# Softmax sums of a whole batch in the PSUM banks of the next batch's k and v projections

## The chip, the core and the metric

The kernel runs on one core of one Trainium2 chip. A core has five engines, each with its own instruction queue that runs in order: TensorE (PE, matrix products; its weight loads are shown apart as PEld), VectorE (DVE, elementwise work), ScalarE (ACT, activation functions and copies), GpSimd (POOL, here almost only the issuer of loads) and SyncE (SP, which issues the other transfers). Sixteen DMA engines move the data that the queues ask for. SBUF is the working memory of 128 partitions; PSUM, of eight banks, takes the results of PE. The metric is the device time of one execution in microseconds, lower is better. Three runs of the kernel before took 473.25, 474.64 and 474.59 us; the median is 474.59.

## What is computed

Linformer attention over 8 batches of 8 heads, 1024 tokens and 64 features a head, followed by a feed-forward block with a squared relu.

```python
k_proj = np.einsum('ks,bhsd->bhkd', E, k)          # 64 projected keys
v_proj = np.einsum('ks,bhsd->bhkd', F, v)
scores = scale * np.matmul(q, k_proj.transpose(0, 1, 3, 2))
attn = np.exp(scores - max); attn = attn / (np.sum(attn, axis=-1, keepdims=True) + 1e-09)
x = np.matmul(attn, v_proj)                        # -> (8192, 512)
h = np.maximum(x @ w_in, 0.0)                      # (8192, 2048)
out = h * h @ w_out                                # (8192, 512)
```

E and F are 64 x 1024, w_in 512 x 2048, w_out 2048 x 512; all inputs and the output are float32. The kernel multiplies in bfloat16 and leaves out the subtraction of the maximum.

## The kernel before, in words

Most of the work is the feed-forward block. Both of its products are done with seven half-size products in place of eight (Strassen's scheme in Winograd's form), with the sums of blocks made on DVE. A batch has two chunks of 512 tokens; the first product of a chunk has four groups (class Group) of seven partial products (p1, p5, p4, p6, p2, p3, p7), each of four matmuls of 256 columns. The generator `firsts` yields after each partial product, `seconds` does the same for the second product (`second_spread`), and `both` puts one of each side by side: a step is four matmuls of a first product and four of a second one. A chunk takes 28 steps, a batch 56.

Attention is threaded between the steps. `plan` maps a step's number to the stages that are put behind that step's products; `on(step, b, name)` enters a method of the batch's Attention object, and in the loop over b the number t = 56 (b - 1) + 28 is the base of the steps in which batch b + 1 is finished and batch b + 2 begun. The order of PE is that of the program text (`manual_schedule`); the order of all other queues is found by a planner, which sorts instructions by when it expects them to be ready. Batches 0 and 1 are done in a different way, before and at the start of this loop (the `chunk_` methods); batches 2 to 7 use these stages:

- `load_q`, `load_kv`: 1 MB each of q, k and v, from memory by POOL's queue, cast to bfloat16 on the way. There is one buffer each for Q, K and V.
- `transpose_q_dma`: Q to qT by a transposing DMA from SP's queue (one qT buffer).
- `project`: sixteen matmuls of 512 columns; those of k go to partitions 0 to 63 of the first bank of a PSUM pair, those of v to partitions 64 to 127 of the second bank. `keep_k` and `keep_v` copy them out, `transpose_k_dma` makes kT.
- `scores(pr)`, for head pair pr of 0 to 3: two matmuls of 512 columns into the PSUM pair, and one exp of 1024 columns on ACT into an expT tile (four buffers).
- `sums_spread(pr)`, for two head pairs at once: eight matmuls with 32 columns of ones as weights, each on its own 64 x 32 piece of the array, into the PSUM pair; Ln and Exp(-x) of 128 x 1024 on ACT give 1/sum in `inv`; and eight DMAs of 32 partitions x 4 KB from SP's queue copy it to the rows where it is needed, in two `rs` tiles.
- `values(pr)`: four matmuls of 64 x 64 x 512 columns into the PSUM pair, and two multiplies by `rs` on DVE into xT.

There is one such PSUM pair (tag "pair", two banks, ps_att) in this part of the program: a stage that writes it waits until the last reader of the stage before is through. `rs` and `inv` share a tag with three buffers.

For batch b + 1 and the next one the loop has: scores 3 at t + 1, sums of pairs 2 and 3 at t + 3, values at t + 7, 10, 20 and 23; Q of b + 2 is loaded from t + 11, behind the last values multiply so far, and transposed at t + 26, k and v of b + 2 are projected at t + 28, its scores 0 to 2 stand at t + 44, 47 and 53, its sums of pairs 0 and 1 at t + 50.

The loads of v of batch 0 stand ahead of the weights' loads in the kernel before and in the changed one.

Of the kernel before, what the change touches and what calls it, by code (L numbers as in the profile page):

```python
# [1 line left out]

# [7 lines left out]
P = 128  # L10
F32 = mybir.dt.float32
BF16 = mybir.dt.bfloat16
AF = mybir.ActivationFunctionType
ALU = mybir.AluOpType
PE = mybir.EngineType.PE
LO, HI = slice(0, 64), slice(64, 128)
# [3 lines left out]
def kernel(  # L20
# [11 lines left out]
    nc = tc.nc  # L32

    B, H, S, D = q.shape
    KP = E.shape[0]
# [4 lines left out]
    NI = 8  # L40
# [4 lines left out]
    TCH = S // 2  # L45
# [10 lines left out]
    const_pool = ctx.enter_context(tc.tile_pool(name="const", bufs=1))  # L56
# [4 lines left out]
    soft_pool = ctx.enter_context(tc.tile_pool(name="soft", bufs=3))  # L61
# [10 lines left out]
    def pair_psum(n, shape, dtype):  # L72
        return pair_pools[n].tile(list(shape), dtype, tag="pair", name="ps_att")

    def att_psum(shape=(P, 2, TCH), dtype=F32):
        turn["att"] += 1
        return pair_psum(turn["att"] % turn["pairs"], shape, dtype)
# [7 lines left out]
    def tokens(src, b, h=slice(None), i=slice(None)):  # L85
        return src[b].rearrange("h (p i) d -> p h i d", i=NI)[:, h, i, :]
# [12 lines left out]
        return t  # L99


    e_f32 = soft_pool.tile([KP, S], F32, tag="rs", name="e_f32")
    nc.sync.dma_start(e_f32[:], E[:])

    k_f32 = soft_pool.tile([P, 2, NI, D], F32, tag="rs", name="k_f32")
    nc.sync.dma_start(k_f32[:], tokens(k, 0, h=slice(0, 2)))

    K0, Q0, V0 = (qkv_pool.tile([P, H, NI, D], BF16, name=n) for n in ("K_sb", "Q_sb", "V_sb"))
# [3 lines left out]
    for g in range(2):  # L112
        h = slice(2 if g == 0 else 4, 4 * g + 4)
# [8 lines left out]
    zeros = const_pool.tile([P, 512], BF16, name="zeros")  # L122
    nc.vector.memset(zeros[:], 0.0)
    ones = const_pool.tile([P, D], BF16, name="ones")
# [7 lines left out]
    for j, (lo, hi) in enumerate(W_IN_PIECES):  # L132
        t = wpool.tile([P, NCB, (hi - lo) * P], BF16, name=f"w_in_{lo}")
# [7 lines left out]
    for j in range(WP):  # L141
        t = wpool.tile([P, fn, DM], BF16, name=f"w_out_{j}")
# [84 lines left out]
    for h in half:  # L227
        nc.scalar.copy(kp[:, h].rearrange("p h a d -> p (h a d)"), zeros[:])
    kT = const_pool.tile([P, H, 2, KP], BF16, name="kT")
    VALUE_QUADS = ((LO, 0, 0, LO), (HI, 1, 1, HI), (HI, 0, 1, LO), (LO, 1, 0, HI))  # L230

    class Attention:
# [30 lines left out]
            nc.scalar.copy(self.vp[HI], view)  # L263
            nc.vector.tensor_copy(self.vp[LO], view)

        def project(self):
            ps = att_psum()
            for i in range(NI):
                f, l = i == 0, i == NI - 1
                nc.tensor.matmul(ps[LO, 0], lhsT=ET[:, i, :], rhs=self.K[:, :, i, :], start=f, stop=l)  # L270
                nc.tensor.matmul(ps[HI, 1], lhsT=FT[:, i, :], rhs=self.V[:, :, i, :], start=f, stop=l)
            self.keep_k(ps[LO, 0], slice(0, H))
            self.keep_v(ps[HI, 1])

        def project_k(self, g):
            ps = bank()
            for i in range(NI):
                nc.tensor.matmul(  # L278
                    ps[LO, 0:C // 2], lhsT=ET[:, i, :], rhs=K0[:, half[g], i, :], start=(i == 0), stop=(i == NI - 1)
                )  # L280
            self.keep_k(ps[LO, 0:C // 2], half[g], nc.scalar.copy if g == 0 else None)
# [45 lines left out]
                    )  # L327
            nc.vector.tensor_copy(self.qT[:, 2 * pr:2 * pr + 2], ps[:])

        def transpose_q_dma(self):  # L330
            nc.sync.dma_start_transpose(
                self.qT[:].rearrange("p h n t -> p (h n) t"), self.Q[:].rearrange("p h i d -> p (h i d)")
            )


        def scores_mm(self, ps, pr, n):
# [6 lines left out]
        def sums_mm(self, ps, e):  # L343
            for o, par, a, r in VALUE_QUADS:
                nc.tensor.matmul(ps[o, par], lhsT=ones[r, :], rhs=e[r, a], start=True, stop=True)  # L345

        def values_mm(self, ps, pr, e):
            for o, par, a, r in VALUE_QUADS:
                nc.tensor.matmul(ps[o, par], lhsT=self.vp[r, 2 * pr + a, :], rhs=e[r, a], start=True, stop=True)  # L349
# [4 lines left out]
            return e  # L354

        def inverse(self, ps):
            rs = soft_pool.tile([P, 2, TCH], F32, tag="rs", name="rs")
            nc.scalar.activation(rs[:], ps[:], AF.Ln)
            nc.scalar.activation(rs[:], rs[:], AF.Exp, scale=-1.0)
            return rs  # L360
# [6 lines left out]
        def sums(self, pr):  # L367

            ps = att_psum()
            for j in range(2):  # L370
                for o, par, a, r in VALUE_QUADS:
                    c = 32 * (2 * a + j)
                    nc.tensor.matmul(
                        ps[c:c + 32, par], lhsT=ones[r, 0:32], rhs=self.e[pr + j][r, a], start=True, stop=True
                    )
            rs = [soft_pool.tile([P, 2, TCH], F32, tag="rs", name="rs") for _ in range(2)]
            nc.scalar.activation(rs[1][:], ps[:], AF.Ln)
            nc.scalar.activation(rs[0][:], rs[1][:], AF.Exp, scale=-1.0)
            nc.scalar.activation(rs[1][:], rs[1][:], AF.Exp, scale=-1.0)
            for j in range(2):  # L380
                for a in range(2):
                    have, lack = 32 * (2 * a + j), 32 * (2 * a + 1 - j)
                    nc.vector.tensor_copy(rs[j][lack:lack + 32], rs[j][have:have + 32])
                self.rs[pr + j] = rs[j]

        def sums_spread(self, pr):

            ps = att_psum()
            for j in range(2):
                for o, par, a, r in VALUE_QUADS:  # L390
                    c = 32 * (2 * a + j)
                    nc.tensor.matmul(  # L392
                        ps[c:c + 32, par], lhsT=ones[r, 0:32], rhs=self.e[pr + j][r, a], start=True, stop=True
                    )
            inv = soft_pool.tile([P, 2, TCH], F32, tag="rs", name="inv")
            nc.scalar.activation(inv[:], ps[:], AF.Ln)
            nc.scalar.activation(inv[:], inv[:], AF.Exp, scale=-1.0)
            for j in range(2):
                rs = soft_pool.tile([P, 2, TCH], F32, tag="rs", name="rs")
                for a in range(2):  # L400
                    have = 32 * (2 * a + j)
                    for to in (64 * a, 64 * a + 32):
                        nc.sync.dma_start(rs[to:to + 32], inv[have:have + 32])
                self.rs[pr + j] = rs

        def values(self, pr, spare=False):

# [3 lines left out]
            else:  # L411
                ps = att_psum()
                ps_x = [ps[:, par] for par in range(2)]
            for o, par, a, r in VALUE_QUADS:
                nc.tensor.matmul(  # L415
# [305 lines left out]
    with tc.manual_schedule(engines={PE}):  # L721
# [31 lines left out]
        plan = {}  # L753

        def at(step, fn, *args, **kwargs):
            plan.setdefault(step, []).append(lambda: fn(*args, **kwargs))
# [13 lines left out]
        atts = {0: att}  # L770
        chunk = {(0, c): Chunk(att, c) for c in range(2)}
# [89 lines left out]
        def both():  # L861
            f, s = firsts(), seconds()
            for _ in f:
                next(s, None)
                yield

        def on(step, b, name, *args):
            at(step, lambda: getattr(atts[b], name)(*args))
# [2 lines left out]
        on(6, 1, "chunk_values", 1, 0)  # L871
        on(12, 1, "chunk_sums", 1, 1)
        on(15, 1, "chunk_values", 1, 1)
        for b in range(B - 1):
            t = 56 * (b - 1) + 28
            if b:
                on(t + 1, b + 1, "scores", 3)
                on(t + 3, b + 1, "sums_spread", 2)
                on(t + 7, b + 1, "values", 0)
                on(t + 10, b + 1, "values", 1)  # L880
                on(t + 20, b + 1, "values", 2)
                on(t + 23, b + 1, "values", 3)
                at(t + 24, lambda b=b: chunk[b + 1, 0].sum_x())
            at(t + 51, lambda b=b: chunk[b + 1, 1].sum_x())
            if b + 2 < B:
                if b:
                    on(t + 11, b + 2, "load_q", lambda b=b: atts[b + 1].done)
                on(t + (26 if b else 32), b + 2, "transpose_q_dma")
                on(t + (28 if b else 36), b + 2, "project")
                on(t + (30 if b else 37), b + 2, "transpose_k_dma")  # L890
                if b + 3 < B:
                    at(t + (32 if b else 37), begin, b + 3)
                    on(t + (32 if b else 37), b + 3, "load_kv", lambda b=b: atts[b + 2].kT_done)
                on(t + (44 if b else 45), b + 2, "scores", 0)
                on(t + (47 if b else 48), b + 2, "scores", 1)
                on(t + (50 if b else 51), b + 2, "sums_spread", 0)
                on(t + (53 if b else 54), b + 2, "scores", 2)
        steps = both()
        run(steps)
        assert not plan, plan  # L900
# [31 lines left out]
```

## Time and profile before

One execution was profiled; it took 473.25 us, with a span of 471.5 us from its first to its last instruction.

| what | value |
|---|---|
| median of three runs | 474.59 us |
| the profiled execution | 473.25 us, span 471.5 us |
| PE busy | 464.1 us, 98% of the span |
| DVE, ACT, POOL busy | 347.6, 297.5, 34.0 us |
| steps in groups' order begin at | about 72.5 us |
| transfers on POOL's queue | 29.23 MB |
| transfers on SP's queue | 37.89 MB |

In the profile's lines, L392 is the sums matmul of `sums_spread`, L396 and L397 its Ln and Exp, L403 its DMAs, L331 the transposing DMA of Q, L304 that of k, L89 a load, L270 and L271 the projection of k and v, L339 the scores, L415 and L419 the matmuls and the multiplies of `values`, L665 and L585 the matmuls of the first and second products, L679 and L675 what DVE and ACT do with a first product, L690 and L557 copies of products on ACT. A line of the timeline has the start and the time in us, the engine (with q for its queue), the source line, the operation, out<-in, the shape and xN for N instructions that follow each other; a line of windows has for each engine the busy time and the number of instructions, and at its end the granted PE clock, the mean busy share of the sixteen DMA engines and GB/s. A line of waits has who waited for whom, the total in us, how often, and the longest.

### The profile page before, as it was taken

The page shows a single profiled execution, that of the slowest core. Times are in us where ns is not written, and L with a number is a line of the kernel's source. Part 1 is how long each engine was busy: PE and PEld are TensorE (multiplying, and loading weights), DVE is VectorE, ACT ScalarE, POOL GpSimd, SP SyncE. Part 2 cuts the span into 40 slices and gives each one's busy share as a digit, 9 for nine tenths or more (in the row PEclk, how much of TensorE's full clock was granted, in tenths as well). Part 3 has the DMA queues.
Part 4 walks back from the last instruction along what each step waited for, and adds up shares of the span by engine and source line. Part 5 has one row for each costly group of instructions (what it writes and reads, how often), then busy time and mean ns, then how long its engine had stood idle before and what let it go on. Part 6 is the DMA issues. An engine that isn't in the chain of part 4 may idle for free.

```text
span 471.5 us, 10107 instructions
## 1 busy us (share of the span) xinstructions
PE 464.1 (98%) x4123; PEld 367.6 (78%) x4141; DVE 347.6 (74%) x595; ACT 297.5 (63%) x484; POOL 34.0 (7%) x47
## 2 busy tenths in 40 slices
PE   8999999999999999999999999999999999999996
PEld 4544677888788787887888888888878878888885
DVE  2469985776968779567895779787796679968571
ACT  4488585887467864677457774568636875555641
POOL 7430100100010000100001000100000000000000
PEclk9999999999999999999999999999999999999999
DMA  9999999895869578785969749695692154101012
GB/s 182 201 205 207 158 206 203 166 217 106 186 138 207 137 141 195 133 171 131 170 180 153 170 98 183 153 197 147 116 219 71 39 132 100 68 24 68 24 69 89
DMA packets 85743, 67.90 MB, mean 144 GB/s; under 512 B 34368, under 2 KB 82240, under 8 KB 85696
## 3 DMA queue, kind: packets, MB, share of 16 engines
q0 software_dynamic: 32208, 29.23, 40.6%
q1 hardware_dynamic: 53344, 37.89, 30.1%
q8 instruction: 32, 0.52, 0.4%
q10 hardware_dynamic: 144, 0.13, 0.1%
q14 instruction: 15, 0.12, 0.1%
HBM read 59.24 MB, written 16.78 MB: 161 GB/s over the span
## 4 chain that ended last, share of the span: by engine, by line
PE 97%; DMA 1%; DVE 1%; ACT 1%; issue 0%; SPq 0%; ACTq 0%; DVEq 0%
PE ps_bank L665 38%; PE ps_second L585 36%; PE ps_bank L502 6%; PE ps_bank L562 3%; PE ps_att L270 3%; PE ps_att L339 2%; PE ps_second L562 2%; PE ps_att L415 2%; DMA k_f<-in_k_dram 1%; PE ps_att L392 1%; PE ps_bank L314 1%; PE ps_att L349 1%; PE ps_att L345 1%; PE ps_bank L220 0%; PE ps_att L289 0%; PE ps_bank L278 0%
## 5 line engine op out<-in xcount | busy, mean ns | idle before, releaser
L154 DVE TENSOR_TENSOR h<-h 128x1024 bf16<-128x1024 bf16 (+1 forms) x170 | 105.4, 645 | 43.9 <-ACT h L675 38.7
L665 PE MATMUL ps_bank<-x_sum,w_in_sum 128*128 128x256 bf16 x672 | 101.1, 273 | 0.1
L665 PEld LDWEIGHTS <-w_in_sum 128*128 128x128 bf16 x896 | 85.5, 98 | 18.9 <-issue 6.3
L585 PEld LDWEIGHTS <-h 128*128 128x128 bf16 x896 | 87.6, 98 | 10.7
L679 DVE CUSTOM_DVE_ANT_0 h<-ps_bank,u 128x512 bf16<-128x512 f32 x112 | 73.8, 685 | 16.2 <-PE ps_bank L665 12.1
L557 ACT COPY u<-ps_bank 128x512 f32<-128x512 f32 x115 | 68.0, 591 | 24.9 <-PE ps_bank L665 23.7
L690 ACT COPY ps_bank<-ps_bank 128x512 f32<-128x512 f32 x56 | 32.0, 571 | 81.5 <-PE ps_bank L665 81.5
L675 ACT ACTIVATE h<-ps_bank 128x512 bf16<-128x512 f32 x112 | 67.9, 607 | 16.7 <-PE ps_bank L665 15.8
L665 PEld LDWEIGHTS <-w_in 128*128 128x128 bf16 x672 | 64.3, 98 | 14.5 <-issue 5.2
L585 PEld LDWEIGHTS <-s 128*128 128x128 bf16 x672 | 65.7, 98 | 7.6
L665 PE MATMUL ps_bank<-xT,w_in 128*128 128x256 bf16 x448 | 67.3, 273 | 0.3
L585 PE MATMUL ps_second<-w_out_sum,s 128*128 128x256 bf16 x448 | 67.2, 273 | 0.0
L585 PE MATMUL ps_second<-w_out_sum,h 128*128 128x256 bf16 x448 | 67.0, 273 | 0.0
L585 PE MATMUL ps_second<-w_out,h 128*128 128x256 bf16 x448 | 64.7, 272 | 0.0
L419 DVE TENSOR_TENSOR xT<-ps_att,rs 128x512 bf16<-128x512 f32 x48 | 30.9, 685 | 13.7 <-PE ps_att L415 13.7
L353 ACT ACTIVATE expT<-ps_att 128x1024 bf16<-128x1024 f32 x32 | 33.1, 1034 | 5.2 <-PE ps_att L339 3.4
L665 PE MATMUL ps_bank<-x_sum,w_in 128*128 128x256 bf16 x224 | 33.7, 273 | 0.3
L665 PE MATMUL ps_bank<-xT,w_in_sum 128*128 128x256 bf16 x224 | 33.6, 273 | 0.1
L154 DVE TENSOR_TENSOR o_sb<-ps_second,u 128x512 f32<-128x512 f32 x29 | 19.9, 685 | 18.7 <-PE ps_second L585 13.6
L585 PE MATMUL ps_second<-w_out,s 128*128 128x256 bf16 x224 | 33.6, 273 | 0.0
L502 PE MATMUL ps_bank<-xT,w_in 128*128 128x512 bf16 x124 | 28.8, 379 | 0.4 <-issue 0.2
L154 DVE TENSOR_TENSOR s<-h 128x1024 bf16<-128x1024 bf16 x32 | 22.0, 691 | 3.7 <-PE ps_second L585 3.0
(97 smaller groups left out, 453.4 us busy)
## 6 DMA issues: line engine op xcount, KB each, us to landing
out_dram<-o_sb SPq DMA_DIRECT2D x63, 256.0 KB, 2.5
rs<-inv SPq DMA_DIRECT2D x96, 128.0 KB, 2.3
K_sb<-in_k_dram POOLq DMA_DIRECT2D x7, 1024.0 KB, 10.2
V_sb<-in_v_dram POOLq DMA_DIRECT2D x7, 1024.0 KB, 14.5
Q_sb<-in_q_dram POOLq DMA_DIRECT2D x6, 1024.0 KB, 11.8
w_out<-in_moe_w_out_dram POOLq DMA_DIRECT2D x4, 512.0 KB, 15.8
Q_sb<-in_q_dram POOLq DMA_DIRECT2D x4, 256.0 KB, 11.0
V_sb<-in_v_dram POOLq DMA_DIRECT2D x2, 512.0 KB, 10.8
```

The source lines that it names most:

```text
L154: return nc.vector.tensor_tensor(out=o, in0=x, in1=y, op=op)
L270: nc.tensor.matmul(ps[LO, 0], lhsT=ET[:, i, :], rhs=self.K[:, :, i, :], start=f, stop=l)
L353: self.done = nc.scalar.activation(e[:], ps[:], AF.Exp, scale=SCALE)
L419: self.done = nc.vector.tensor_tensor(out=self.xT[:, pr, :, par], in0=ps_x[par].rearrange("p (c t) -> p c t", c=2), in1=rs[:, par].rearran ...
L502: nc.tensor.matmul(ps[:], lhsT=w_in_blk(cb, fb), rhs=self.xT[:, cb, self.c].rearrange("p a t -> p (a t)"), start=(cb == 0), stop=(cb == NC ...
L557: nc.scalar.copy(u[:], ps)
L562: nc.tensor.matmul(ps[:, i * HM:(i + 1) * HM], lhsT=self.h_form(n, fb)[:, i * P:(i + 1) * P], rhs=w_out_form(n, fb), start=fresh and i == ...
L585: nc.tensor.matmul(ps[:, i * HM:(i + 1) * HM], lhsT=self.h_form(n, fb)[:, i * P:(i + 1) * P], rhs=w_out_form(n, fb), start=fresh and i == ...
L665: nc.tensor.matmul(ps[:, j * HC:(j + 1) * HC], lhsT=w_in_form(n, cb, 2 * self.g + j), rhs=self.chunk.x_form(n, cb), start=fresh and j == 0 ...
L675: nc.scalar.activation(self.out(kh, a), ps[:], AF.Relu)
L679: nc.vector._custom_dve(TENSOR_ADD_SAT, out=self.out(kh, a), in0=ps[:], in1=more[:], s0=3.0e38, s1=0.0)
L690: nc.scalar.copy(self.chain[:], self.first[:])
```

## The change

The sums of all four pairs of a batch are now made at once. Their sixteen matmuls use a weight tile `pick` that has ones in eight of its 32 columns, another eight for each pair, and add up in PSUM, so that a group of 32 partitions holds eight copies of each pair's sums. They go to the halves of the PSUM pair that the projection leaves free: partitions 64 to 127 of the first bank, 0 to 63 of the second. For batches 3 to 6 they follow the sixteen projection matmuls of the next batch in the same stage (step t - 10); for batches 2 and 7 they stand alone. ACT does Ln in two halves of 64 x 512 and one Exp of 128 x 512. `spread` then makes a pair's `rs` tile with four DMAs, each of which reads eight partitions of 2 KB eight times over and writes 64 partitions: for pairs 0 and 1 from SP's queue, at step t - 9, for pairs 2 and 3 from POOL's, at the steps of values 0 and 1, which free the `rs` buffers. The tag of `rs` now has two buffers, and `inv` one of its own.

The steps move with it: scores of batch b + 2 at t + 29, 36, 40 and 44, all in one batch's first half; values at t + 7, 11, 17 and 21; Q is transposed at t - 9, on SP behind the spreads, K of the next batch too; Q of b + 3 is entered at t + 12 and k, v at t + 18. The steps of batches 2 and 3 are written out ahead of the loop (values of batch 2 at t + 9, 12, 19 and 23, with t = 28).

```diff
-    k_f32 = soft_pool.tile([P, 2, NI, D], F32, tag="rs", name="k_f32")
+    k_f32 = soft_pool.tile([P, 2, NI, D], F32, tag="rs", bufs=2, name="k_f32")
...
+    pick = const_pool.tile([P, H // 2, 32], BF16, name="pick")
+    nc.scalar.copy(pick[:].rearrange("p m k -> p (m k)"), zeros[:, 0:P])
+    for m in range(H // 2):
+        nc.scalar.copy(pick[:, m, 8 * m:8 * m + 8], ones[:, 0:8])
...
-        def project(self):
+        def project(self, sums=None):
             ps = att_psum()
...
+            if sums:
+                sums.sums_all(ps)
+                sums.log(1)
             self.keep_k(ps[LO, 0], slice(0, H))
             self.keep_v(ps[HI, 1])
+            if sums:
+                sums.log(0)
+                sums.inverse_all()
...
-        def sums_spread(self, pr):
...
+        def sums_all(self, ps=None):
+            ps = att_psum() if ps is None else ps
+            for m in range(H // 2):
                 for o, par, a, r in VALUE_QUADS:
-                    c = 32 * (2 * a + j)
+                    c = HI.start * (1 - par) + 32 * a
                     nc.tensor.matmul(
-                        ps[c:c + 32, par], lhsT=ones[r, 0:32], rhs=self.e[pr + j][r, a], start=True, stop=True
+                        ps[c:c + 32, par], lhsT=pick[r, m], rhs=self.e[m][r, a],
+                        start=m == 0, stop=m == H // 2 - 1, skip_group_check=True,
                     )
...
-                for a in range(2):
-                    have = 32 * (2 * a + j)
-                    for to in (64 * a, 64 * a + 32):
-                        nc.sync.dma_start(rs[to:to + 32], inv[have:have + 32])
...
+        def log(self, par):
+            rows = (HI, LO)[par]
+            nc.scalar.activation(self.inv[rows], self.ps_sums[rows, par], AF.Ln)
+
+        def inverse_all(self):
+            nc.scalar.activation(self.inv[:], self.inv[:], AF.Exp, scale=-1.0)
+
+        def spread(self, pr):
+            rs = soft_pool.tile([P, 2, TCH], F32, tag="rs", bufs=2, name="rs")
+            for o, par, a, r in VALUE_QUADS:
+                c = HI.start * (1 - par) + 32 * a + 8 * pr
+                self.spread_done = (nc.sync if pr < 2 else nc.gpsimd).dma_start(rs[o, par], self.inv[c:c + 8].unsqueeze(1).broadcast_to((8, 8, TCH)))
+            self.rs[pr] = rs
...
+        on(4, 2, "transpose_q_dma")
+        at(5, begin, 3)
+        on(5, 3, "load_q")
+        on(8, 2, "project")
+        on(9, 2, "transpose_k_dma")
+        on(10, 3, "load_kv", lambda: atts[2].kT_done)
+        for pr in range(4):
+            on((18, 20, 22, 24)[pr], 2, "scores", pr)
+            if pr < 2:
+                on(27, 2, "spread", pr)
+        plan[27].insert(0, lambda: atts[2].sums_alone())
+        on(42, 3, "project")
+        on(43, 3, "transpose_k_dma")
+        on(28, 3, "transpose_q_dma", 2)
+        at(32, begin, 4)
+        on(32, 4, "load_q")
+        on(44, 4, "load_kv")
         for b in range(B - 1):
             t = 56 * (b - 1) + 28
...
+            if b > 1:
+                if b + 2 < B:
+                    at(t - 10, lambda b=b: atts[b + 2].project(atts[b + 1]))
+                    on(t - 9, b + 2, "transpose_k_dma")
+                else:
+                    on(t - 10, b + 1, "sums_alone")
+                for pr in range(2):
+                    on(t - 9, b + 1, "spread", pr)
+                if b + 2 < B:
+                    on(t - 9, b + 2, "transpose_q_dma", b + 1)
+                    if b + 3 < B:
+                        at(t + 12, begin, b + 3)
+                        on(t + 18, b + 3, "load_kv", lambda b=b: atts[b + 1].done)
+                        on(t + 12, b + 3, "load_q")
+            for pr in range(4):
+                on(t + (9, 12, 19, 23)[pr] if b == 1 else t + (7, 11, 17, 21)[pr], b + 1, "values", pr)
+                if pr < 2:
+                    on(t + ((9, 12) if b == 1 else (7, 11))[pr], b + 1, "spread", pr + 2)
             at(t + 24, lambda b=b: chunk[b + 1, 0].sum_x())
             if b + 2 < B:
...
+                for pr in range(4):
+                    on(t + (29, 36, 40, 44)[pr], b + 2, "scores", pr)
```

`sums_alone` is sums_all, log(1), log(0) and inverse_all in a row, for the batches that have no projection beside them.

## The prediction

> **What bounds the kernel now.** I read the page first (engine shares and chain), then the waits of TensorE, then its timeline at one softmax-sum stage.
>
> ```profile
> span 471.5 us, 10107 instructions
> ...
> PE 464.1 (98%) x4123; PEld 367.6 (78%) x4141; DVE 347.6 (74%) x595; ACT 297.5 (63%) x484; POOL 34.0 (7%) x47
> ...
> PE 97%; DMA 1%; DVE 1%; ACT 1%; issue 0%; SPq 0%; ACTq 0%; DVEq 0%
> ```
>
> ```profile
> PE ps_bank L220 <- DVE zeros L123: 1.2, 1, 1.2
> PE ps_bank L211 <- DVE e_bf L723: 0.6, 1, 0.6
> PE ps_att L339 <- DVE kT L301: 0.2, 1, 0.2
> ```
>
> All that TensorE (PE) waits for lies in the first microseconds; behind them it is the bound without a break. So time can leave only where PE has less to do, and the time that ACT, DVE or a queue saves is worth nothing; what a later wait adds to PE is paid in full.
>
> ```profile
> 149.88 0.60 PE L665 MATMUL ps_bank<-xT,w_in 128*128 128x256 bf16 x4
> 150.32 0.60 PE L585 MATMUL ps_second<-w_out,s 128*128 128x256 bf16 x4
> 150.85 0.41 PE L392 MATMUL ps_att<-expT,ones 64*32 64x512 bf16 x8
> 151.19 0.39 PE L665 MATMUL ps_bank<-x_sum,w_in_sum 128*128 128x256 bf16 x2
> ```
>
> Starts count here: four main matmuls take 0.44 us (149.88 to 150.32), so a step of eight takes 0.87. The sums stage holds PE from 150.76 to 151.19: 0.43 us, of which 0.09 is lost on entry and about 0.10 on exit. Its eight matmuls use eight different pieces of the array (two halves of rows, four groups of 32 columns) and run in one pass.
>
> Then I looked at the transfers that bring 1/sum to the multiply: issues, shares of the DMA engines by stretch, and the waits of POOL's queue.
>
> ```profile
> rs<-inv SPq DMA_DIRECT2D x96, 128.0 KB, 2.3
> ...
> Q_sb<-in_q_dram POOLq DMA_DIRECT2D x6, 1024.0 KB, 11.8
> ```
>
> ```profile
> qT<-Q_sb SPq DMA_TRANSPOSE x6, 5.6
> ```
>
> ```profile
> 209.15 5.00 SPq L403 DMA_DIRECT2D rs<-inv  x8
> ```
>
> ```profile
> 2.50:3.30 0.80, 0.80 (x3) 0.25 (x2) 0.00 (x0) 0.67 (x2) 0.80 (x3) 1.00 0.79 277
> 210.40:215.40 5.00, 5.00 (x53) 4.12 (x50) 4.09 (x7) 3.60 (x7) 0.00 (x0) 1.00 0.91 205
> ```
>
> ```profile
> POOL Q_sb L89 <- DVE xT L419: 146.4, 5, 30.7
> ```
>
> Eight spreads go out in 5.0 us, 0.63 each, and land 2.3 us after issue. While they run, the engines are 0.91 busy for 205 GB/s, 14 GB/s for a busy engine; the loads from memory at 2.5 us get 277/16/0.79 = 22. So a spread that reads 32 partitions is already held back by something other than the DMA engines. The last line shows that the Q load was made to wait, up to 30.7 us, for a multiply: it never stood in front of the spreads of the same batch.
>
> **The change, part by part.**
>
> *Sums on PE.* Removed: 12 stages of 0.43 = 5.2 us. Added: six groups of 16 matmuls. All four pairs use the same four pieces of the array, so I count four passes in a row of 0.213 (the pitch of the k/v projection: 129.23, 129.44, 129.65), 0.85 a batch. For batches 3 to 6 they follow the projection without an entry or exit (0 to 0.1 for the change of shape); batches 2 and 7 stand alone, +0.2. Sum 4 x 0.85..0.95 + 2 x 1.05 = 5.5 to 5.9: +0.3 to +0.7, I take +0.5. If the passes overlapped as the eight of before do, 16 would take half, 6 x 0.43 less = -2.6; they share pieces, so I leave that to a rival.
>
> *ACT.* 12 x (1.02 + 1.06) = 25 us go; 6 x 3 operations of 512 columns at 0.6 (the rows of that length: 571 to 607 ns) come, 11 us. No PE wait names ACT: 0. The five copies that build pick (about 1 us) lie in the 2.7 us in which ACT waits for the first k.
>
> *SP and POOL.* SP issues 48 spreads instead of 96; POOL gets 48, at 0.56 to 0.87 (its shortest and longest load issues). The sums of the next batch, scores and transposes move by up to 36 steps; their PE time moves unchanged. Two rs buffers in place of three delay nothing early: chunk sums re-use a buffer some ten us after its multiply.
>
> *The spreads themselves.* Same bytes, but each DMA now reads 8 partitions eight times over in place of 32 once. Low end: as before, 0.63 a spread. High end: if the limit goes with the partitions read, 205/32 = 6.4 GB/s each gives 51 GB/s, 131 KB / 51 = 2.5 us. That busy engines slow down on 32 partitions puts it above the low end; neighbours in the queue read different halves and may overlap, so it is below the high one. I take the middle, 1.5.
>
> [...] No run so far shows a spread from 8 partitions.
>
> *Order of the queues.* In the changed program's own order SP issues kT, eight spreads, then qT of the next batch; POOL's load of Q (it waits for qT to land, one Q buffer) stands before the four spreads of pair 2, in batches 3 to 5. For batch 2 it stands behind three of them. POOL waits in order, so those spreads cannot start before Q does, and run behind its 1 MB. On DVE the multiply that waits for rs holds up everything after it; on PE the next values waits for that multiply, since there is one ps_att pair.
>
> *One middle batch*, in us from the start of its projection-and-sums stage (step t-10). PE: stage 2.8 (1.85 for the projection, 0.95), then values 0 to 3, 17, 21, 27 and 31 steps on with 0.44 for each values: at 17.6, 21.5, 27.2, 31.1. ACT's order puts the second Ln behind the copy of a product four steps later (ending 6.4); Ln, a kept copy and Exp at 0.6 each: 1/sum at 8.3. Spreads issue 8.4 to 13.4; qT lands 5.6 later, or some 4.5 after the last spread has run. Q lands 10.5 after qT (K and Q rows: 10.2, 11.8, the latter beside spreads). Four spreads of pair 2 follow. Values 3 can start on time if they are there at 30.4 (multiply 0.69).
> - 0.63 a spread: qT 19.0, Q 29.5, spreads 32.0: 1.6 lost.
> - 1.5: eighth spread 21.9, qT 26.4, Q 36.9, spreads 42.9: 12.5 lost, and some 0.5 on pair 3, whose spreads come behind: 13.
> - 2.5: 29.9, 34.4, 44.9, 54.9: 24.5, and 3 to 4 on pair 3: 28.
>
> Three batches (3, 4, 5): 5, 39, 84. Batch 2, the same sum with ten steps from sums to values: 2, 9, 21. Batches 6 and 7, with no Q load: 0, 1, 16. With PE's +0.5: **+7, +50, +121**. Against the profiled execution (473.25; its span 471.5) that is 480, 523, 594. The median shown, 474.59, is 1.3 above it; on its scale I predict **524 us**.
>
> **Rivals.**
> 1. *Spreads as fast as before, Q still in front*: 477 to 490, about 481. For it: same bytes, same kind of transfer. Against: 14 against 22 GB/s for a busy engine.
> 2. *All hidden*: POOL's Q load lands in 8.6 us, as the quickest K load did (86.62 to 95.26), qT in 5.6: spreads at 30, no loss, +0.3 to +0.7: 475. It needs every term at its best, three times.
> 3. *Faster*: the 16 sums matmuls of a batch finish in the time of eight; -2.6 and nothing lost: 472. It decides only if pair 2 is there by 30.4 as well. Against: same pieces of the array.
> 4. *The full limit by partitions*: about 595, the end of the main case.
>
> [...]
>
> **How the numbers follow.** Main case, slow spreads behind Q (490 to 600): 0.57. Rival 1: 0.26; rival 2: 0.13; rival 3: 0.04. The range goes from the low edge of rival 1 to the main case's upper end, 476 to 600; it leaves out rivals 2 and 3, 0.17. A change within 0.3% (1.4 us) cannot be told from none; rival 2 is that: same 0.13, faster 0.04, slower 0.83.
>
> **What would show it.** Right: waits of DVE on transfers into rs, the longest at values 2 and 3 of batches 2 to 5; PE idle before values and before L665 products, in four stretches some 55 us and more apart; a landing of rs from POOL over 10 us, and from SP over 4; DMA GB/s in the spreads' stretch under 205. Wrong: rs landing in 2 to 3 us with DVE never waiting on DMA; sums matmuls that run more than four at a time; a Q load that lands before the first multiply of its window, or is not in front.

## The result, and the profile after

The changed kernel takes 550.43 us (median of four runs, 546.08 to 551.10) against 474.62 us for the kernel before in the same comparison: a ratio of 1.158, 95% interval 1.151 to 1.165. The prediction was 524 us with a range of 476 to 600: the sign and the mechanism are right, the amount is 26 us short. In the changed program the lines are L691 and L611 for the matmuls of the first and second products, L441 and L445 for the matmuls and multiplies of `values`, L405 for the sums matmuls, L423 for the spreads, L343 for the transposing DMA of Q, L275 for the projection, L705 for what DVE does with a first product. The profiled execution took 550.73 us. Of the runs below, one execution with 32 source partitions (509.00 us) counts as slow, being over 1.5% above the fastest, and is left out of that run's median and ratio.

First the page: span, busy shares, the granted clock by slices, the chain that ended last.

```profile
span 548.9 us, 10159 instructions
...
PE 480.8 (88%) x4118; PEld 375.8 (68%) x4141; DVE 350.5 (64%) x595; ACT 286.0 (52%) x483; POOL 61.4 (11%) x95
...
PEclk9999999998599996999869999699996999999999
...
PE 62%; DMA 20%; SPq 7%; DVE 5%; ACT 3%; issue 2%; POOL 1%; DVEq 0%; POOLq 0%; ACTq 0%
```

PE's share fell from 98% to 88%, and the chain that was 97% PE now has 27% of transfers and of SP's queue in it. Yet PE is busy 16.7 us longer than before, although its work grew by 0.8 us: the granted clock dips to 5 or 6 tenths in five slices.

The waits of PE, of DVE and of POOL's queue (total, times, longest, in us):

```profile
PE ps_att L441 <- DVE xT L445: 36.1, 4, 10.4
PE ps_bank L691 <- DVE h L705: 21.5, 5, 14.2
PE ps_att L275 <- DVE xT L445: 2.9, 1, 2.9
```

```profile
DVE xT L445 <- DMA rs<-inv: 66.3, 15, 12.9
```

```profile
POOL Q_sb L89 <- DMA qT<-Q_sb: 93.1, 3, 61.2
...
POOL rs L423 <- DMA Q_sb<-in_q_dram: 10.9, 2, 5.5
```

Before, PE waited for nothing after the first microseconds. Now it waits for multiplies (and for relu work that stands behind them on DVE), and the multiplies wait for the spreads. Batch 3 shows the whole chain. From the timeline of POOL, SP, DVE and PE:

```profile
189.20 7.09 SPq L343 DMA_TRANSPOSE qT<-Q_sb  x1
...
198.93 0.88 POOL L89 DMA_DIRECT2D Q_sb<-in_q_dram  x1 [61.24 <-DMA qT<-Q_sb]
...
200.12 3.94 POOL L423 DMA_DIRECT2D rs<-inv  x7 [0.32 <-ACT u L583]
209.43 0.56 POOL L423 DMA_DIRECT2D rs<-inv  x1 [5.36 <-DMA Q_sb<-in_q_dram]
210.56 0.69 DVE L445 TENSOR_TENSOR xT<-ps_att,rs 128x512 bf16<-128x512 f32 x1 [9.44 <-DMA rs<-inv]
...
212.50 0.64 PE L441 MATMUL ps_att<-expT,vp 64*64 64x512 bf16 x4 [10.01 <-DVE xT L445]
```

The load of Q goes out when qT has landed, the spreads of pairs 2 and 3 sit behind its 1 MB, the multiply of pair 2 waits 9.4 us for them, and values 3 waits 10.0 us for that multiply.

Why qT is late is in the windows (us and instructions of PE, PEld, DVE, ACT, POOL; then granted clock, busy share of the DMA engines, GB/s). The first is the stretch of the eight spreads on SP, the third is the end of the wait just shown.

```profile
180.50:190.50 10.00, 10.00 (x94) 8.56 (x92) 8.52 (x14) 5.37 (x11) 0.00 (x0) 1.00 0.44 91
203.00:208.00 5.00, 0.00 (x0) 0.00 (x0) 0.00 (x0) 0.00 (x0) 1.06 (x2) 0.96 1.18 207
208.00:213.00 5.00, 0.50 (x4) 0.14 (x4) 2.44 (x5) 0.00 (x0) 0.56 (x2) 0.50 0.93 152
213.00:217.50 4.50, 4.50 (x25) 3.17 (x22) 3.92 (x9) 1.16 (x2) 1.83 (x2) 0.50 0.52 78
217.50:222.00 4.50, 4.50 (x42) 3.98 (x40) 2.54 (x5) 1.78 (x3) 0.00 (x0) 0.96 1.16 209
```

The spreads move 91 GB/s where those of before moved 205. And after the wait PE runs 25 matmuls in 4.5 us at a granted clock of 0.50, against 42 in the next 4.5 us. That second loss was in no step of the prediction.

Where the time went: the waits are PE's start-to-start distances beyond the pitch of the shape; the loss is the distance between the starts of two projection-and-sums stages, less 55.4 us, which the same distance is before (for batch 6, between the starts of two groups of sums matmuls, less the 53.6 of the run without spreads below); the half clock is what is left.

| batch | waits, us | loss, us | half clock, us |
|---|---|---|---|
| 2 | 17.5 | 19.3 | 1.8 |
| 3 | 11.4 | 13.8 | 2.4 |
| 4 | 12.3 | 16.3 | 4.0 |
| 5 | 12.3 | 13.9 | 1.6 |
| 6 | 8.7 | 11.5 | 2.8 |
| 7 | 0 | 0 | 0 |

(Batch 2 has another order; its loss is worked out from all excess distances of PE behind 73 us, 87.4 us less the 12.6 of before, less the other batches.) The waits are 62 us, the half clock 12.6, the longer sums 0.8: 75.6 of the 77.4 us between the two spans. Of the rest, 1.5 us lies in front of the first projection of batch 1 (55.59 against 54.13 us); in other runs below that start varies from 54.1 to 56.0, with no relation to their times.

### The profile page after: what moved, and what is told of

Same layout as the page of the kernel before. It is cut to its first block, busy times and chain, and to the rows that moved or that the text cites. A ratio compares the mean times of both kernels' runs of the same rounds, so it can differ in the third digit from the quotient of the medians.

```text
span 548.9 us, 10159 instructions
## 1 busy us (share of the span) xinstructions
PE 480.8 (88%) x4118; PEld 375.8 (68%) x4141; DVE 350.5 (64%) x595; ACT 286.0 (52%) x483; POOL 61.4 (11%) x95
## 4 chain that ended last, share of the span: by engine, by line
PE 62%; DMA 20%; SPq 7%; DVE 5%; ACT 3%; issue 2%; POOL 1%; DVEq 0%; POOLq 0%; ACTq 0%
PE ps_bank L691 22%; PE ps_second L611 21%; DMA rs<-inv 15%; SPq L423 7%; PE ps_bank L528 5%; PE ps_bank L588 3%; DMA qT<-Q_sb 3%; PE ps_att L351 2%; PE ps_att L275 2%; PE ps_second L588 2%; DVE xT L445 1%; PE ps_att L405 1%; DMA out_dram<-o_sb 1%; DVE h L705 1%; PE ps_att L441 1%
## 5 line engine op out<-in xcount | busy, mean ns | idle before, releaser
L691 PE MATMUL ps_bank<-x_sum,w_in_sum 128*128 128x256 bf16 x672 | 103.9, 278 | 21.8 <-DVE h L705 21.5
L691 PEld LDWEIGHTS <-w_in_sum 128*128 128x128 bf16 x896 | 88.0, 99 | 40.8 <-issue 25.6
L611 PEld LDWEIGHTS <-h 128*128 128x128 bf16 x896 | 87.6, 98 | 10.6
L445 DVE TENSOR_TENSOR xT<-ps_att,rs 128x512 bf16<-128x512 f32 x48 | 32.0, 688 | 82.0 <-DMA rs<-inv 66.3
L701 ACT ACTIVATE h<-ps_bank 128x512 bf16<-128x512 f32 x112 | 67.6, 604 | 21.8 <-PE ps_bank L691 20.1
L705 DVE CUSTOM_DVE_ANT_0 h<-ps_bank,u 128x512 bf16<-128x512 f32 x112 | 73.0, 685 | 8.2 <-PE ps_bank L691 4.3
L691 PEld LDWEIGHTS <-w_in 128*128 128x128 bf16 x672 | 65.3, 100 | 17.4 <-issue 7.6
L611 PEld LDWEIGHTS <-s 128*128 128x128 bf16 x672 | 68.9, 103 | 10.8
L691 PE MATMUL ps_bank<-xT,w_in 128*128 128x256 bf16 x448 | 69.1, 278 | 0.1
L611 PE MATMUL ps_second<-w_out_sum,s 128*128 128x256 bf16 x448 | 68.1, 275 | 0.0
L611 PE MATMUL ps_second<-w_out_sum,h 128*128 128x256 bf16 x448 | 67.0, 273 | 0.0
L611 PE MATMUL ps_second<-w_out,h 128*128 128x256 bf16 x448 | 64.7, 272 | 0.0
L423 POOL DMA_DIRECT2D rs<-inv x48 | 27.0, 578 | 147.3 <-DMA out_dram<-o_sb 56.5
L441 PE MATMUL ps_att<-expT,vp 64*64 64x512 bf16 x96 | 11.2, 458 | 36.1 <-DVE xT L445 36.1
L611 PE MATMUL ps_second<-w_out,s 128*128 128x256 bf16 x224 | 39.2, 305 | 0.0
L691 PE MATMUL ps_bank<-x_sum,w_in 128*128 128x256 bf16 x224 | 35.9, 286 | 0.3
L89 POOL DMA_DIRECT2D Q_sb<-in_q_dram x12 | 10.2, 851 | 218.5 <-DMA out_dram<-o_sb 110.0
L691 PE MATMUL ps_bank<-xT,w_in_sum 128*128 128x256 bf16 x224 | 33.6, 273 | 0.0
```

Of the source, the lines that this page charges most:

```text
L423: self.spread_done = (nc.sync if pr < 2 else nc.gpsimd).dma_start(rs[o, par], self.inv[c:c + 8].unsqueeze(1).broadcast_to((8, 8, TCH)))
L445: self.done = nc.vector.tensor_tensor(out=self.xT[:, pr, :, par], in0=ps_x[par].rearrange("p (c t) -> p c t", c=2), in1=rs[:, par].rearran ...
L611: nc.tensor.matmul(ps[:, i * HM:(i + 1) * HM], lhsT=self.h_form(n, fb)[:, i * P:(i + 1) * P], rhs=w_out_form(n, fb), start=fresh and i == ...
L691: nc.tensor.matmul(ps[:, j * HC:(j + 1) * HC], lhsT=w_in_form(n, cb, 2 * self.g + j), rhs=self.chunk.x_form(n, cb), start=fresh and j == 0 ...
L701: nc.scalar.activation(self.out(kh, a), ps[:], AF.Relu)
L705: nc.vector._custom_dve(TENSOR_ADD_SAT, out=self.out(kh, a), in0=ps[:], in1=more[:], s0=3.0e38, s1=0.0)
```

## The experiments

Theory: two things together make the loss, (a) spreads that read eight neighbouring partitions are slow, which delays qT and so Q, and (b) Q's load stands in front of the spreads of pairs 2 and 3. The rivals: (a) alone, (b) alone, or something else that the change moved.

**Rows four partitions apart.** The eight equal rows of a pair no longer lie together.

```
-    nc.scalar.copy(pick[:, m, 8 * m:8 * m + 8], ones[:, 0:8])
+    nc.scalar.copy(pick[:, m, m:32:4], ones[:, 0:8])
...
-    c = HI.start * (1 - par) + 32 * a + 8 * pr
-    self.spread_done = (...).dma_start(rs[o, par], self.inv[c:c + 8].unsqueeze(1).broadcast_to((8, 8, TCH)))
+    c = HI.start * (1 - par) + 32 * a
+    self.spread_done = (...).dma_start(rs[o, par], self.inv[c + pr:c + 32:4].unsqueeze(1).broadcast_to((8, 8, TCH)))
```

> The eight equal rows of 1/sum of a head pair are put four partitions apart (c + pair, c + pair + 4, ...) in place of eight neighbours; bytes, number of source partitions (8), descriptors, queues and their order stay. Theory A (the spreads are held back by where their eight source partitions lie): a spread on SP goes back from the 1.31 us of the changed kernel to about 0.65, eight of them end some 5 us after the first issue, qT lands about 20 us after the start of the projection-and-sums stage, Q about 30, pair 2 about 32; 1 to 3 us of TensorE's time lost in each of batches 3 to 5, no stretch at half the granted clock, 476 to 490 us. Theory B (reading so few partitions, or repeating a read eight times, is slow wherever they lie; or only 8 of 16 DMA engines take part): the spread stays at 1.2 to 1.4 us, 543 to 553 us.

Measured: 508.11 us, ratio 1.0735 (1.0684 to 1.0786). Issues of spreads on SP (shortest, median, longest in ns), first in the changed kernel and then here, and a window of the spreads' stretch here:

```profile
L423 SPq DMA_DIRECT2D rs<-inv x48: 605/1310/2251, 105.2 to 460.5; - x48
```

```profile
L423 SPq DMA_DIRECT2D rs<-inv x48: 604/604/783, 104.0 to 411.5; - x48
```

```profile
170.20:175.00 4.80, 4.80 (x47) 4.31 (x44) 4.73 (x9) 2.75 (x5) 0.00 (x0) 1.00 0.56 155
```

The same bytes from the same number of partitions go at 155 GB/s in place of 91, so where the rows lie is a cause, and it is worth 42 us. But 508 is not the 476 to 490 that was expected. The issues are back at 0.65 us each; the packets are not: between the first and the seventh eighth of the bytes a spread takes 0.90 us here and 1.35 in the changed kernel (batches 3 to 6 of both). In batch 2 of this run it takes 0.65, as in the kernel before, and a window of it shows 201 GB/s:

```profile
108.50:110.50 2.00, 2.00 (x21) 1.80 (x19) 0.76 (x2) 0.57 (x1) 0.00 (x0) 1.00 0.52 201
```

The edit is the same in all batches, so something else holds the later ones at 0.90; no run here shows what. In batch 3, counted from the start of the stage at 159.39: SP's spreads are out at +14.2, Q goes out at +21.8 and lands at +32.2, the last spread of pair 2 lands at +35.9, where +30.4 was needed. 5.4 us are lost there (4.9 to 8.6 in batches 2 to 5), and each of these waits is followed by a stretch at half the clock.

**Q behind the spreads.** Only (b) is undone.

```
     def load_q(self, behind=None):
-        self.Q = load_batch("Q_sb", q, self.b, behind)
+        with tc.issue_after(atts[behind].spread_done.ins) if behind else nullcontext():
+            self.Q = load_batch("Q_sb", q, self.b)
...
-    on(t + 12, b + 3, "load_q")
+    on(t + 12, b + 3, "load_q", b + 1)
```

(The load of batch 4 likewise, at step 41 behind the spreads of batch 2.)

> The load of the next Q is put behind the eight spreads of pairs 2 and 3 on POOL's queue (batches 2 to 5); the spreads keep their eight neighbouring partitions. Theory A (slow spreads and the Q load in front of them cost together): the spreads of pairs 2 and 3 then run beside the transpose of Q as in batch 6, which lost 8.7 us; batches 3 to 5 fall from about 12.3 to 8.7 lost, batch 2 from 17.5 to about 9: 528 to 536 us. Theory B (the Q load costs nothing, the slow source is all): 545 to 552 us. Theory C (the Q load in front is nearly all of it): 476 to 490 us.

Measured: 535.56 us, ratio 1.128 (1.121 to 1.135), the top of theory A's range. Issue times of the transposing DMA of Q, in the changed kernel and then here:

```profile
L343 SPq DMA_TRANSPOSE qT<-Q_sb x6: 4057/8843/15517, 81.3 to 399.3; - x6
```

```profile
L344 SPq DMA_TRANSPOSE qT<-Q_sb x6: 4231/14790/15650, 80.5 to 381.1; - x6
```

```profile
rs<-inv POOLq DMA_DIRECT2D x48, 128.0 KB, 14.5
```

With Q out of the way the spreads of pairs 2 and 3 go out when their multiply is done, and then run beside the transpose: they land after 14.5 us in the median, and the transpose holds SP for 14.8 us where it took 4.0 before. Batches 3 to 5 lose 9.4 to 14.3 us. Undoing (b) alone turns one wait into another.

**Both.** The two edits above together.

> Both edits: rows four partitions apart, and the Q load behind the spreads. If these two are the whole of the loss, all six batches have their 1/sum in time and what is left is the longer sums stage on TensorE (0.8 us over the kernel before): 474.5 to 478 us. If something else in the change costs time (moved scores and transposes, two rs buffers in place of three, the halves of the multiply and relu work on VectorE), over 480 us.

Measured: 476.49 us, ratio 1.0055 (1.0037 to 1.0072). The page and PE's waits:

```profile
PE 466.7 (98%) x4118; PEld 369.8 (78%) x4141; DVE 348.4 (73%) x595; ACT 286.2 (60%) x483; POOL 61.5 (13%) x95
...
PEclk9999999999999999999999999999999999999999
```

```profile
PE ps_att L352 <- DMA kT<-kp: 1.2, 1, 1.2
```

This is the expected case: PE has no long wait left and its clock is full. One edit saves 42 us, the other 15, both together 74: the two causes feed each other. Slow spreads delay qT and with it the Q that stands in front; once Q is out of the way, they meet the transpose instead. What is left over the kernel before is 2.9 us between the medians. In the profiled execution (477.69 us) it is 4.4, of which the longer sums are 0.8, the wait for kT just shown 1.2 and the later start of batch 1's projection (56.02 against 54.13 us) 1.9.

**No spread at all.** The multiplies read a constant.

```
-    rs = soft_pool.tile(...)
-    ... four dma_start of inv into rs
+    self.rs[pr] = fixed_rs[:].unsqueeze(1).broadcast_to((P, 2, TCH))
```

> No 1/sum is spread: the multiplies read a constant instead (the division by the softmax sums is left out of batches 2 to 7; sums, Ln and Exp are still computed, and qT waits for the Exp in place of the last spread). Both theories on the spreads say that every stall and every stretch at half the clock comes from the spreads, so that only the sums stage is left: the kernel before + 0.8 us, 474.5 to 476.5 us. If the moved steps or the joined stage stall TensorE by themselves, over 478 us.

Measured: 474.87 us, ratio 1.0025 (1.0008 to 1.0042): no wait of PE over 1 us is left behind the first microseconds, so all of the stalls and all of the half clock come from the spreads. Of the 1.3 us that remain, 0.8 is the longer sums stage (0.97 us when joined to the projection, 1.07 alone, against two stages of 0.43 in each batch of before).

**32 partitions, and eight two apart.** Two more sources, to see by what the rate goes. The first reads 32 neighbours twice (c is now the start of the group of 32):

```
-    self.inv[c:c + 8].unsqueeze(1).broadcast_to((8, 8, TCH))
+    self.inv[c:c + 32].unsqueeze(1).broadcast_to((32, 2, TCH))
```

> The spreads of the changed kernel read 32 neighbouring partitions twice in place of eight neighbours eight times (the 32 rows hold the sums of all four pairs, so every token is divided by a sum of the wrong pair in part of its columns: that part of the computation is wrong, bytes and packets are not). Q stays in front. If what counts is how far apart the source partitions lie (theory A), this is the run with rows four partitions apart again: a spread in 0.65 us, 504 to 512 us. If the number of partitions read or the repeated read counts as well, spreads take less than 0.60 us each and the time is below 500 us.

The second puts a pair's eight rows two partitions apart (`inv[c + pr % 2:c + 16:2]`, with c at one half of the group of 32 for pairs 0 and 1 and at the other for pairs 2 and 3, and `pick` to match).

> The eight equal rows of a pair lie two partitions apart (they reach over 16 partitions in place of 8 or 32); nothing else. If the rate goes with the stretch of partitions that a spread reaches, it lies between the changed kernel (1.31 us a spread on SP) and the rows four apart (0.65): 0.65 to 0.95 us each, because two neighbours in the queue can run together, and 508 to 530 us. If only direct neighbours collide, 0.65 us and 504 to 512 us.

Measured: 501.82 us (ratio 1.0602, 1.0541 to 1.0662) and 515.97 us (ratio 1.0892, 1.0853 to 1.0932). A window of the spreads' stretch of each, in this order:

```profile
170.00:174.00 4.00, 4.00 (x39) 3.59 (x37) 3.93 (x8) 2.19 (x5) 0.00 (x0) 1.00 0.76 200
```

```profile
171.00:175.00 4.00, 4.00 (x40) 3.58 (x38) 3.93 (x8) 2.16 (x4) 0.00 (x0) 1.00 0.48 152
```

Together with the changed kernel and the first run there are four points, all in batch 3: eight neighbours 91 GB/s, eight over 16 partitions 152, eight over 32 partitions 155, 32 neighbours 200. So the stretch of partitions that is reached matters up to 16, and in these batches the number of partitions read matters as well (0.66 us a spread with 32 rows). Theory A was too simple, and neither forecast of the first run's time came: 501.8 us lies between theory A's 504 to 512 and its rival's "below 500", since Q still stands in front.

The DMA engines' mean busy share differs as well, 0.44 to 0.56 with eight rows and 0.76 with 32; how many of the sixteen take part is not shown. The share alone does not set the rate: in the first run 0.56 moved 155 GB/s in batch 3, and 0.52 moved 201 in batch 2.

The time does not follow the spreads' own rate alone. Rows two and four apart move nearly the same GB/s, and yet two apart takes 8 us longer: the transpose behind the spreads holds SP for 6.0 to 8.2 us there in batches 2 to 6, against 5.0 to 5.5 with rows four apart and 7.1 to 15.5 with eight neighbours. The source rows thus cost a second time, in the transpose; how they do it is not shown.

**The kernel before with a narrow source.** The price of (a) where nothing else of the change is.

```
-    nc.sync.dma_start(rs[to:to + 32], inv[have:have + 32])
+    nc.sync.dma_start(rs[to:to + 32], inv[have:have + 8].unsqueeze(1).broadcast_to((8, 4, 2, TCH)))
```

> The kernel before with one edit: each spread reads the first eight of its 32 equal rows four times, in place of the 32 once; its order, its queues and its sums stay. Theory A: a spread takes 1.2 to 1.5 us in place of 0.63, eight of them some 11 us in place of 5; pairs 1 and 3 come up to 1 or 2 us late at twelve places, 476 to 495 us, far from the changed kernel's 550, since nothing stands in front of them. If the source partitions are harmless by themselves: 0.63 us a spread and the time of before.

Measured: 586.31 us, ratio 1.239 (1.235 to 1.244): 113 us slower, far beyond both theories. The spreads go out every 2.4 us once the queue is full, and the window shows 57 GB/s:

```profile
176.00:184.00 8.00, 7.98 (x75) 6.40 (x74) 7.47 (x12) 4.74 (x9) 0.00 (x0) 1.00 0.48 57
```

```profile
PE ps_att L415 <- ACT inv L396: 65.4, 6, 11.6
```

The rate was missed because of the order, as the next run shows: here two spreads that follow each other read the same eight rows. And the place of the loss was missed: the three rs buffers are shared by `inv` and two rs tiles, the Ln of the second stage waits for a buffer that slow spreads still read, and the sums hold the only ps_att pair until that Ln, so values 0 waits 11 us in each batch. (The profile puts the Ln's wait down to a store, though no store touches the Ln's tiles. In the second stage of batch 3 the last packet of the spreads in front ends at 193.06 us, and the Ln starts at 193.66.)

**The same with another order.** No two neighbours in the queue read the same rows.

```
-    for a in range(2): ... for to in (64 * a, 64 * a + 32): dma_start
+    for to in (0, 32): ... for a in range(2): dma_start into rs[64 * a + to: ...]
```

> As the run that narrows the source in the kernel before (586 us; there a spread and the next one read the same eight partitions, and the spreads went out every 2.4 us), but the order of the eight is changed so that no two neighbours in the queue read the same partitions. Theory A (one spread from eight neighbours takes 2.4 us by itself; neighbours in the queue that read other partitions run beside it, which is why the changed kernel shows 1.3 to 1.5): 1.3 to 1.6 us a spread, the ring of three rs buffers comes free earlier, 485 to 525 us. Theory B (the spread from eight partitions takes 2.4 us in this kernel whatever its neighbour reads): 575 to 590 us.

Measured: 537.39 us, ratio 1.134 (1.130 to 1.139). The issue times (ns):

```profile
L403 SPq DMA_DIRECT2D rs<-inv x96: 682/1640/2856, 101.0 to 505.4; - x96
```

```profile
L403 SPq DMA_DIRECT2D rs<-inv x96: 682/1012/2277, 101.1 to 457.1; - x96
```

The first line is the run before this one, the second this one. In a group of eight the third to the eighth issue follow each other by 1.65, 2.3, 1.05, 1.55 and 1.05 us, 1.5 in the mean, as in the changed kernel: theory A's rate, and theory B is out. The time was set too low again: the wait on the rs ring fell from 11 us a batch only to 6.4, and each is followed by a half-clock stretch of 6.8 us (10.2 in batch 2).

**PE kept busy in the wait.** Is the half clock a cost of its own?

```
 def values(self, pr, spare=False):
+    if pr == 3 and 3 <= self.b <= 6:
+        fill = bank(n=turn["bank"] + 4)
+        for _ in range(37):
+            nc.tensor.matmul(fill[:], lhsT=zeros[:, 0:P], rhs=zeros[:], start=True, stop=True)
```

> The changed kernel with 37 matmuls of zeros (512 columns, into a bank that is free there; 7.9 us at the full clock) in front of values 3 of batches 3 to 6, where TensorE waits 7.7 to 10.5 us: its work grows, its idle time there shrinks to 3 us or less. Theory A (the stretches at half the granted clock come from TensorE's long idle times and cost time on top of them): no half clock in these batches, about 2.4 us saved in each, 538 to 543 us. Theory B (the half clock has another cause, or costs nothing because the spreads end the wait anyway): 548 to 556 us.

Measured: 544.17 us (542.10 to 546.08), ratio 1.148 (1.144 to 1.153). The window around the restart in batch 4, where the changed kernel ran at 0.50:

```profile
277.00:282.00 5.00, 2.04 (x17) 1.10 (x16) 3.19 (x6) 0.20 (x1) 0.76 (x1) 1.00 0.71 118
282.00:290.00 8.00, 8.00 (x74) 6.99 (x72) 7.86 (x15) 4.82 (x9) 1.08 (x2) 1.00 0.91 144
```

The kernel does more and takes 6 us less. The half clock is gone from batches 4 to 6 (a stretch of 3.4 us stays in batch 3), and the distances between stages in the four batches shrink by 0.6, 2.6, 1.4 and 1.2 us, 5.8 in all; 9.6 was expected. So theory A's mechanism is shown and its size is not: in each of the last three batches the waits that stay and the fill together are 0.1 to 1.7 us more than the waits that they replace. The two intervals of the ratios overlap a little, so the sign of the saving rests on these distances as much as on the medians. The rest of the difference between the two profiled spans lies in batch 2, where nothing was changed.

**All spreads on SP.** The run with both edits, and `nc.sync` for all four pairs.

> As the run with both edits (476.5 us), and the spreads of pairs 2 and 3 issued by SP, behind qT, in place of POOL. If POOL's queue as such costs nothing, and only what stood in front of the spreads there did: the same, 475 to 478 us. If SP now holds its stores and kT behind spreads that wait for a multiply: 479 to 490 us. If POOL's slower landings (4.0 us against 2.6) cost something: 473.5 to 475 us.

Measured: 484.96 us, ratio 1.025 (1.021 to 1.029): the second case. PE's waits in the profiled execution (488.72 us, one of the two longest of six):

```profile
PE ps_bank L692 <- DVE h L706: 5.0, 4, 2.7
PE ps_att L352 <- DMA kT<-kp: 4.8, 1, 4.8
```

On SP the spreads of pairs 2 and 3 stand behind qT and hold kT and the stores back while they wait for their multiply. Against the run with both edits that is 2 points of the ratio, some 9 us, which issuing half of the spreads on POOL was worth. So it was not POOL's queue that cost time in the changed kernel but what stood in front of the spreads there.

A sums stage in which two pairs use the two halves of rows at once was not tried. None of these versions is faster than the kernel before.

## Why the prediction was right or wrong

- *What bounds the kernel, and that a later wait is paid in full*: this was right. PE's waits and slower matmuls make up 75 of the 77 us between the two spans, and the 11.5 us less work of ACT (297.5 to 286.0; 14 were forecast) bought nothing.
- *PE +0.5*: measured +0.8. The four passes come in a row, 0.216 us apart, as counted; with entry and exit a batch's sums take 0.97 us joined and 1.07 alone. Rival 3 (half the passes) is out.
- *1.5 us a spread*: it is 1.35 between the first and the seventh eighth of the bytes. The 1.5 was the middle of two bounds and not worked out, so that it came this close is partly luck. The last packet of the eighth spread came at +24.4 from the stage's start, where the sum had +21.9, because its last packets run among those of the transpose. (The sum's 21.9 holds a further 1.5 us, from the first issue to its first packet, that it does not name; 1.3 was measured.) The two bounds were both found: 0.66 with 32 rows, and 2.4 in the kernel before with a narrow source. There 131 KB / 2.4 us = 55 GB/s, near the 51 that the prediction estimated from 205 / 32 for each partition read; but the number read alone does not set the limit, since eight rows four apart moved 155. The changed kernel's 97 (131 / 1.35) is nearly twice the 55: in it neighbours in the queue read different halves of the partitions, and the two runs that differ in the order alone show that such neighbours run beside each other (2.4 us a spread against 1.5). The prediction's "may overlap" was this; two at a time, each in the 2.4 us of that run, give an estimate of 1.2 us.
- *A middle batch*: the step times are in the table.

| step, us from the stage's start | predicted | measured, batch 3 |
|---|---|---|
| first spread issued | 8.4 | 8.8 |
| last packet of eighth spread | 21.9 | 24.4 |
| qT landed, Q issued | 26.4 | 29.1 |
| Q landed | 36.9 | 39.3 |
| pair 2 spread (its second multiply starts) | 42.9 | 41.9 |
| waits of PE | 13 | 11.4 |

Two sizes were off and cancelled, which is luck: qT was 2.7 us later, and the four spreads behind Q took 2.6 us in place of 6.0 (POOL's spreads there landed 0.6 us apart). The waits of the three batches are 36 us where the sum had 39.

- *Batch 2, 9 us*: the waits are 17.5. The failed term is the 4.5 us from the last spread to qT. Three spreads of pair 2 went out on POOL before Q, as the order said, and ran beside the transpose; that held SP for 12.2 us, and Q went out only at 132.1 us.
- *Batches 6 and 7, 1 us*: the waits are 8.7 and 0. The term was costed on the absence of a Q load alone. In batch 6 POOL's spreads, issued at 400.2 us, landed from 410.9 to 418.4 beside a transpose of 15.5 us; in batch 7 there is no transpose, and they landed in 5.0 to 7.6 us. The run with Q behind shows the same transpose, 14.5 to 15.7 us long, in batches 2 to 6.
- *The clock*: the prediction had no term for it, and it took 12.6 us. All three cases of the sum were worked out at the full clock, so each batch with long waits was priced 1.6 to 4.0 us too low. With batch 2 (+8.5) and batch 6 (+7.7), less the 3 us that the middle batches were under, this is the 26 us.
- *Rival 1, 477 to 490*: the run that reads 32 partitions comes nearest to its situation, with 0.66 us a spread and Q in front, and took 502. So the rival's own price was too low: in batch 3 Q went out 21.4 us after the stage's start, where its sum had 19.0, and landed at 32.0, where it had 29.5; 4.3 to 7.2 us were lost in each of batches 2 to 5, where the sum had some 1.6 to 2, and the clock came on top. *Rival 2* needed Q out of the way and fast spreads; both edits together come nearest to it, 476.5 for 475 forecast. *Rival 4* is what the kernel before did with the narrow source, in another place.
- *What would show it*: it came as listed (DVE's waits on rs, PE's idle time before values and L691, 91 GB/s under 205), but in five stretches, not four. Landings from POOL have a median of 9.6 us, up to 16.6; for those from SP the profile gives none.

## What to carry to other kernels

Price a small spread by where its source rows lie and by what its neighbours in the queue read, not by its bytes or by the issue times: the same 128 KB took 0.66, 0.90, 1.35 or 2.4 us here, and replicating rows at a distance of four partitions in place of side by side cost nothing. Price the transfer behind them too: the transpose took 4.0 to 15.7 us by what was beside it. A transfer that waits in order (the load of Q behind qT, up to 61.2 us in the changed kernel) delays everything queued behind it, so look at each queue's own order and ask what the next obstacle is; undoing one of two such causes gave back 15 or 42 of 74 us. And add the clock to every TensorE wait of some 4 us or more: here it took 1.6 to 4.0 us in each of batches 2 to 6.

## What the runs showed of the hardware

- TensorE's granted clock fell to 0.50 in or just after every one of the 38 waits of 3.9 us and longer that the changed kernel and the runs above show. Of the six between 3.0 and 3.8 us one had it (3.7) and five had not (one of them also 3.7). Of the shorter waits most had not, but three had: 2.2 and 2.3 us in the kernel before with the narrow source, and 2.8 us, right behind another wait, in the run with all spreads on SP. The stretches lasted 3.41, 6.83, 10.24 and, after the longest wait, 17.07 us; matmuls of 256 columns then followed each other by 213 ns in place of 109, and the full clock came back 2.9 to 6.1 us after the restart. Why two waits of 3.7 us differ, and why the three shorter ones had it, is not shown.
- A transposing DMA slowed with the spreads beside it: SP needed 4.0 us for it before (median), 5.2 where the spreads came from rows four apart, 7.1 to 9.9 in batches 3 to 5 of the changed kernel, behind SP's spreads from eight neighbours, and 12 to 15.7 beside spreads from eight neighbours that POOL issued. The spreads slowed with it: those of POOL landed 14.5 us after issue (median) in the run with Q behind, and in 5.0 to 7.6 us in batch 7 of the changed kernel, which has no transpose. In batch 6 of the changed kernel, from 402 to 411 us, all transfers together moved 62 GB/s in the mean; from 412 to 413 us, alone, the transpose moved 288.
- POOL's eighth spread behind a load of Q was issued only when Q had landed (the 5.36 us in the timeline above), and the same in the middle batches of the run with the rows four apart.
